# A first half of the next unit's hidden product, and an output tile, placed between two block products of a fused attention and two-MoE kernel

## The chip, the cores and the metric

One NeuronCore of a Trainium2 chip runs the whole program. The metric is the device time of one execution in microseconds (us); the median of three runs of the kernel before is 636.27 us.

## The reference, cut to what matters

The program is three layers in a row: banded attention (a plain and a dilated window), a mixture of four experts, and a layer with a rational activation. The change lies in the second layer:

```python
def _moe_ref(x, domain_probs, w1, w2):
    N, D = x.shape                       # 1152 tokens, 512
    E = w1.shape[0]                      # 4 experts, 1024 hidden each
    p = domain_probs / (domain_probs.sum(-1, keepdims=True) + 1e-09)
    out = np.zeros((N, D), dtype=np.float32)
    for e in range(E):
        h = np.maximum(x @ w1[e], 0.0)
        out += p[:, e:e + 1] * (h @ w2[e])
    return out
```

## The kernel before, in words

The 4096 hidden values of the four experts are cut into 16 **units** of 256; two units make a **group** (`g` from 0 to 7, units `u = 2g` and `u + 1`). The 1152 tokens are three **chunks** of 384 (c = 0, 1, 2), or nine output tiles of 128 (t = 0 to 8; chunk c holds tiles 3c to 3c + 2). Every float32 factor is split into a high and a low part, and a product is three products: high by high, high by low, low by high.

For each unit and chunk the kernel forms a hidden product (128 hidden values by 384 tokens per PSUM bank, two banks), takes ReLU, and splits it into `hh` (ScalarE, L485) and `hl` (VectorE, L489). For each group and output tile it then multiplies `hh` and `hl` with both units' `w2` (an output tile, twelve matmuls of L513) and adds the result to `acc`: in most groups ScalarE scales the tile into `part` (L543) and a DMA issued by GpSimd adds it (L544); in the last group VectorE does both (L546).

**Chunk 0** of a unit is computed plainly: `h_paced` (L898) issues two banks with `h_bank` (L461, twelve matmuls of L467 each), then the ReLU. **Chunks 1 and 2 together** are computed from groups 1 on by seven block products instead of eight (a scheme in the manner of Strassen), in class `Blocks` (L924). Each block product is six matmuls of L935 and accumulates into PSUM. A unit has two PSUM tiles of two banks: `yz` for chunk 1 and `vz` for chunk 2. The steps are:

- `first` into `yz` bank 1, copied to bank 0 by ScalarE (L974); `fifth` into a bank of its own, copied to `p5` (L981); `sixth` onto `yz` bank 1;
- `sum_up`, which asks VectorE for the sum of `yz` bank 1 and `p5` into `vz` bank 0 (the add of L961);
- `seventh` onto `yz` bank 1, after which a second add of L961 writes `vz` bank 1 from `yz` bank 1 and `p5`;
- `second` onto `yz` bank 0; `third` onto `vz` bank 0, then the ReLU of chunk 2; `fourth` onto `yz` bank 1, then the ReLU of chunk 1.

The loop of L1023 writes the order of a group out by hand. Of the group's first unit, `a`, the second add is followed by `second` of `a`, then by `first` of the other unit, `b`, and only then by `third` and `fourth` of `a`. Of the second unit, `b`, the order is `fifth`, `sixth`, `sum_up`, output tiles 0, 1, 2 of this group (0 and 1 in group 7), `seventh`, `second`, `third`, `fourth`, with nothing between. The next group begins with both banks of chunk 0 for its first unit and the output tiles 6, 7, 8 of the group before.

TensorE's order is the program's. The other engines' work is woven in by a planner (class `Pace`, L756 to L806): each TensorE step advances a model clock with `passed` (L787) by its cost in `COST`; work with a due time (`later`), such as the adds and the low halves of the ReLU, is issued once the clock has passed it, and the gaps are filled with preparation (`behind`: splitting weights, forming sums of weight blocks) and with the conversion of the third layer's weights from float64. `settle` issues what a step needs before it goes on. Hidden PSUM tiles come from a pool of two (`psh`) or, where `last` is True, from a third one; output tiles take turns in two banks (`pso`). In the add of a unit:

```python
            def add(self, n, wait=0.2):
                out, y, p5 = self.place(n), self.place(1), self.p5
                later(
                    wait, COST["add"], ("add", self.u),
                    lambda: nc.vector.tensor_tensor(out=out, in0=y, in1=p5, op=ALU.add),
                )
```

After group 7 a list written out by hand, `DENSE`, orders the third layer.

Of the kernel before, what the change touches and what calls it, by code (L numbers as in the profile page):

```python
# [95 lines left out]
COST = dict(h=2.09, p=1.045, o=2.74, osum=0.78, relu=1.0, add=0.59, split=0.68, sums=0.42, bits=0.41, both=1.15, token=1.0)  # L96
# [5 lines left out]
def body(ctx, tc, qkv, mask, dp, w1, w2, w1d, w2d, coef, out):  # L102
# [15 lines left out]
    def h_tile(last=None):  # L118

        count[0] += 1  # L120
        last = third and count[0] % 3 == 0 if last is None else last
        pool = third[0] if last else psh
        return pool.tile([128, 2, 512], F32, tag="h", name="ps_h")
# [67 lines left out]
    def weight(store, u, n):  # L191

        return (store[u][:, i].rearrange("p (k f) -> p k f", k=n) for i in range(2))
# [267 lines left out]
    def h_bank(u, c, i, ps, ks=range(4)):  # L461
        wh, wl = weight(w1s, u, 4)
        xh, xl = xt[c]
        for k in ks:
            f = slice(i * 128, (i + 1) * 128)
            for n, (a, b) in enumerate(((wh, xh), (wh, xl), (wl, xh))):
                nc.tensor.matmul(  # L467
                    ps[:, i, :TC], lhsT=a[:, k, f], rhs=b[:, k],
                    start=k + n == 0, stop=k + n == 5,
                )  # L470
# [46 lines left out]
    def o_bank():  # L517
        return pso.tile([128, 512], F32, tag="o", name="ps_o")
# [41 lines left out]
    class Rational:  # L560
# [53 lines left out]
        def high(self):  # L614
            self.hh, self.hl = new_h(self.u, self.c)
            nc.scalar.copy(self.hh, self.u1)  # L616
# [6 lines left out]
    with tc.manual_schedule():  # L623
# [73 lines left out]
        def fill(u, c, i):  # L697
            if i == 0:
                ps_h[u, c] = h_tile()
            h_bank(u, c, i, ps_h[u, c])  # L700
# [6 lines left out]
        def small_loads():  # L707
# [9 lines left out]
            g=small_loads,  # L717
# [44 lines left out]
        def run_due(n=0):  # L762
            ready, cost, _, f = Pace.due.pop(n)
            Pace.dv = max(Pace.dv, ready) + cost if cost else Pace.dv
            f()

        def run_prep():
            ready, cost, _, f = Pace.prep.pop(0)
            Pace.dv = max(Pace.dv, ready) + cost if cost else Pace.dv
            f()  # L770
# [16 lines left out]
        def passed(us):  # L787

            Pace.pe += us
            while Pace.due and min(Pace.due)[0] <= Pace.pe:  # L790
                n = Pace.due.index(min(Pace.due))
                fill(Pace.due[n][0])
                run_due(n)
            fill(Pace.pe)

        def later(wait, cost, key, f):
            Pace.due.append((Pace.pe + wait, cost, key, f))

        def settle(key):
            while any(d[2] == key for d in Pace.due):  # L800
                run_due(Pace.due.index(min(Pace.due)))
            while any(d[2] == key for d in Pace.prep):
                run_prep()

        def behind(cost, key, f, wait=0.0):
            Pace.prep.append((max(Pace.pe, Pace.dv) + wait, cost, key, f))  # L806

        def act_then(key, act, low, cost):

            def both():  # L810
                act()
                n, dv = 0, 0.0
                while not Pace.conv[0] and n < len(Pace.prep) and dv < 1.0 and Pace.prep[n][1]:
                    dv += Pace.prep[n][1]
                    n += 1
                Pace.prep.insert(n, (Pace.dv + 1.0, cost, key, low))
            return both
# [70 lines left out]
        def tokens_later(src, high, low, key="tokens", then=None):  # L888
# [6 lines left out]
                    then()  # L895
            behind(0.0, key, act_then(key, act, dve, COST["token"]))

        def h_paced(u, c, last=None):  # L898
            settle(("w1", u))
            ps = h_tile(last)  # L900
            for i in range(2):
                h_bank(u, c, i, ps)
                passed(COST["h"])
            high, low = relu_parts(u, c, ps)
            high()
            later(1.1, COST["relu"], ("h", u, c), low)

        def o_paced(g, t, wait=0.0):
            for v in range(2):
                settle(("h", 2 * g + v, t // 3))  # L910
                settle(("w2", 2 * g + v))
            ps = o_bank()
            for v in range(2):
                o_half(g, t, v, ps)
            passed(COST["o"])
            if by_dma(g, t):
                if wait:
                    later(wait, 0.0, ("o", g, t), lambda: o_sum(g, t, ps))
                else:
                    o_sum(g, t, ps)  # L920
            else:
                later(0.2, COST["osum"], ("o", g, t), lambda: o_sum(g, t, ps))
# [100 lines left out]
        for g in range(NG1):  # L1023
            u = 2 * g
            again = g + 1 in BLOCKED
            o = lambda *at: [(o_paced, *i) for i in at]
            if g == 0:
                later(0.0, COST["osum"], ("o", 0, 3), lambda: o_sum(0, 3, ps_2[3]))
                token_sums()
                tokens_later(temp[0], *(t[:, 0] for t in tt))  # L1030
                sums_later(2)
                sums_split_later(2, 1)
                o_paced(0, 4)
                o_paced(0, 5)
                for v in range(2):
                    h_paced(v, 2)
                tokens_later(temp[2], *(t[:, :2] for t in xt[2]), "first")
                sums_split_later(2, 0)
                tokens_later(temp[1], *(t[:, 1] for t in tt), "second")
                sums_later(3)  # L1040
                tokens_later(temp[3], *(t[:, 2] for t in tt), "third", begin_conversion)
                continue
            a, b = (Blocks(v) for v in (u, u + 1))
            w2_loads = (load_w2, u + 2), (load_w2, u + 3)
            free = [(load_w1, u + 3)] * (g > 1) + [w2_loads[0]] * (g == 1) + [w2_loads[1]]
            free = [(weights_free, *free)] if again else []
            run = lambda g, *ts: [o_paced(g, t, 1.5 * (n == 2)) for n, t in enumerate(ts)]

            def next_sums():
                if again:  # L1050
                    sums_later(u + 2)
                    sums_split_later(u + 2, 1)
                    split_later(w2s, "w2", u + 2)
                    split_later(w1s, "w1", u + 3)
                else:
                    loads((load_w1, u + 3))

            if g == 1:
                sums_split_later(u + 1, 1)
                split_later(w1s, "w1", u + 2)  # L1060
                a.first(False)
                o_paced(0, 6)
                a.sixth()
                a.fifth()
                a.sum_up(0.8, False)
                o_paced(0, 7)
                a.seventh()
                a.second()
                sums_split_later(u + 1, 0, free)
                o_paced(0, 8)  # L1070
            else:
                for v in (u, u + 1):
                    new_h(v, 0)
                h_paced(u, 0, False)
                sums_split_later(u + 1, 1)
                split_later(w2s, "w2", u + 1)
                if again:
                    split_later(w1s, "w1", u + 2)
                run(g - 1, 6, 7, 8)
                a.first(False)  # L1080
                h_paced(u + 1, 0, True)
                a.fifth()
                a.sixth()
                a.sum_up(0.2, False)
                run(g - 1, 3, 4)
                sums_split_later(u + 1, 0, free)
                o_paced(g - 1, 5, 1.5)
                a.seventh()
                a.second()
            b.first(True)  # L1090
            a.third()
            a.fourth()
            next_sums()
            b.fifth()
            b.sixth()
            b.sum_up(0.2, False)
            run(g, *range(3 if again else 2))
            b.seventh()
            b.second()
            b.third()  # L1100
            b.fourth()
            if g == 1:
                Window.spare[:] = [None, lone[:, 0], lone[:, 1]]
            if again:
                sums_split_later(u + 2, 0, [(loads, (load_w1, u + 4))])
                sums_later(u + 3)
            else:
                loads(*w2_loads, (load_w1, u + 4), (load_w1, u + 5))
# [144 lines left out]
        def of(name):  # L1253
# [3 lines left out]
            h=bank, o=second, O=lambda *a: second(*a, of="h"), z=sum_up, x=turn, X=x_high, Y=x_low, W=x_whole,  # L1257
# [5 lines left out]
            i=load_w1, j=load_w2, k=load_sums,  # L1263
# [112 lines left out]
```

## Time and profile before

| | |
|---|---|
| median of 3 runs | 636.27 us (635.47 to 637.51) |
| the profiled execution | 636.8 us |
| its span, first to last instruction | 635.0 us |
| mean granted TensorE clock | 0.999 of full speed |
| TensorE matmul busy | 622.0 us, 98% of the span |
| VectorE busy | 522.6 us, 82% |
| ScalarE busy | 371.5 us, 58% |
| GpSimd busy | 88.1 us, 14% |

Times in the rows are from the start of the span; the profiled execution is 1.8 us longer than its span. PE is TensorE's matmul, PEld its weight load, DVE VectorE, ACT ScalarE, POOL GpSimd, SP SyncE (SPq is its DMA queue). A line such as L961 is the line of the kernel that issued the instruction.

### The profile page before, as it was taken

What the parts mean: (1) busy time and instruction counts of PE and PEld (TensorE: products, weight loads), DVE (VectorE), ACT (ScalarE), POOL (GpSimd) and SP (SyncE); (2) the same over time, 40 slices, a digit from 0 to 9 for tenths busy, and PEclk for the clock granted to TensorE, in tenths of its full rate; (3) what the DMA queues carried; (4) which work ended last, traced back from release to release, by engine and by line L of the source; (5) the groups of instructions that cost most, each with busy time, mean ns of one, the idle gap of its engine ahead of it and who ended that gap; (6) DMA issues with size and microseconds to landing.
All of it is one profiled execution on the core that took longest, in us unless ns stands there. A gap on an engine that the chain in (4) does not pass through costs nothing.

```text
span 635.0 us, 9851 instructions
## 1 busy us (share of the span) xinstructions
PE 622.0 (98%) x3726; PEld 554.6 (87%) x3728; DVE 522.6 (82%) x788; ACT 371.5 (58%) x682; POOL 88.1 (14%) x103
## 2 busy tenths in 40 slices
PE   7999999999999999999999999999999999999997
PEld 4888898899899899899899889888998889899886
DVE  7687488789888888888898888438898899899894
ACT  6787625355554554464555555127688686877760
POOL 2223330011111112112112111000000002111110
PEclk9999999999999999999999999999999999999999
DMA  9965302259778869879868878950331563572333
GB/s 264 311 171 168 111 11 67 100 138 258 230 214 239 242 196 265 239 211 247 253 188 244 248 207 225 316 199 10 124 133 38 180 212 95 116 239 51 67 78 105
DMA packets 39535, 111.28 MB, mean 175 GB/s; under 512 B 4256, under 2 KB 5024, under 8 KB 37440
## 3 DMA queue, kind: packets, MB, share of 16 engines
q1 hardware_dynamic: 29104, 92.14, 43.9%
q0 software_dynamic: 9936, 18.09, 16.3%
q8 instruction: 29, 0.48, 0.3%
q10 hardware_dynamic: 448, 0.43, 0.3%
q14 instruction: 18, 0.15, 0.1%
HBM read 67.13 MB, written 25.43 MB: 146 GB/s over the span
## 4 chain that ended last, share of the span: by engine, by line
PE 97%; DVE 1%; DMA 1%; ACT 0%; issue 0%
PE ps_o L513 45%; PE ps_h L467 21%; PE ps_h L935 14%; PE ps_h L1232 7%; PE ps_o L935 2%; PE ps_v L431 2%; PE ps_s L417 1%; PE ps_h L513 1%; DMA qk<-in_qkv_dram 1%; PE ps_s L362 1%; PE ps_h L1166 1%; DVE ps_h L961 1%; PE ps_h L655 1%; PE ps L362 0%; DVE xl L893 0%
## 5 line engine op out<-in xcount | busy, mean ns | idle before, releaser
L513 PE MATMUL ps_o<-w,hh 128*128 128x512 f32 (+1 forms) x848 | 228.7, 391 | 0.3 <-DVE xl L455 0.3
L513 PEld LDWEIGHTS ps_o<-w,hh 128*128 128x128 f32 x848 | 157.0, 188 | 29.8 <-DVE xl L455 0.7
L513 PE MATMUL ps_o<-w,hl 128*128 128x512 f32 (+1 forms) x424 | 131.0, 390 | 0.1
L467 PE MATMUL ps_h<-xh,w 128*128 128x384 f32 x464 | 125.2, 338 | 0.0
L513 PEld LDWEIGHTS ps_o<-w,hl 128*128 128x128 f32 x424 | 79.4, 188 | 17.6 <-DVE hl L489 0.6
L467 PEld LDWEIGHTS ps_h<-xh,w 128*128 128x128 f32 x464 | 84.4, 188 | 1.0
L544 POOL DMA_DIRECT2D acc<-part x51 | 45.1, 884 | 264.0 <-ACT part L543 262.1
L467 PE MATMUL ps_h<-xl,w 128*128 128x384 f32 x232 | 77.7, 335 | 0.0
L543 ACT ACTIVATE part<-ps_o,p_sb 128x512 f32<-128x512 f32 x51 | 35.1, 688 | 54.8 <-PE ps_o L513 24.3
L485 ACT ACTIVATE hh<-ps_h 128x768 fp32r<-128x768 f32 x48 | 38.9, 812 | 41.0 <-PE ps_h L935 22.8
L489 DVE SCALAR_TENSOR_TENSOR hl<-ps_h,hh 128x768 fp32r<-128x768 f32 x48 | 45.4, 953 | 12.7 <-ACT hh L485 11.9
L467 PEld LDWEIGHTS ps_h<-xl,w 128*128 128x128 f32 x232 | 43.6, 188 | 0.4
L1151 POOL DMA_DIRECT2D acc<-part x18 | 15.6, 867 | 200.3 <-ACT part L1150 199.7
L271 ACT ACTIVATE x<-x 128x512 f32<-128x512 f32 x32 | 21.8, 681 | 21.4 <-DVE t L268 21.4
L935 PE MATMUL ps_h<-t,sw 128*128 128x384 f32 x168 | 34.0, 337 | 0.0
L833 DVE TENSOR_TENSOR w<-raw,w 128x512 fp32r<-128x512 f32 x48 | 32.8, 683 | 0.9 <-ACT w L829 0.9
L396 ACT ACTIVATE pr<-pr,mx 128x80 f32<-128x80 f32 (+1 forms) x84 | 29.8, 358 | 5.9 <-DVE mx L390 4.6
L935 PEld LDWEIGHTS ps_h<-t,sw 128*128 128x128 f32 x168 | 29.9, 188 | 1.2
L580 DVE SCALAR_TENSOR_TENSOR sq<-sq,absb,ab 128x768 f32<-128x768 f32 x24 | 24.2, 1013 | 7.9 <-ACT sq L569 6.7
L935 PE MATMUL ps_h<-xh,w 128*128 128x384 f32 x104 | 29.8, 336 | 0.0
L829 ACT CAST w<-raw 128x512 fp32r<-128x512 f32 x48 | 28.6, 614 | 0.0
L616 ACT CAST hh<-u 128x768 fp32r<-128x768 f32 x24 | 19.9, 838 | 13.4 <-DVE u L610 13.2
(158 smaller groups left out, 1132.2 us busy)
## 6 DMA issues: line engine op xcount, KB each, us to landing
acc<-part POOLq DMA_DIRECT2D x69, 256.0 KB, 5.5
raw<-in_w_dram SPq DMA_DIRECT2D x32, 512.0 KB, 6.3
w<-w SPq DMA_DIRECT2D x14, 1024.0 KB, 6.1
w<-lone SPq DMA_DIRECT2D x18, 512.0 KB, 4.9
x<-in_w1d_dram SPq DMA_DIRECT2D x16, 512.0 KB, 5.1
x<-in_w2d_dram SPq DMA_DIRECT2D x16, 512.0 KB, 5.2
w<-w SPq DMA_DIRECT2D x14, 512.0 KB, 4.5
sw<-sw SPq DMA_DIRECT2D x12, 512.0 KB, 7.5
```

The costliest lines, as they stand in the source:

```text
L396: nc.scalar.activation(pr[:, j, i], pr[:, j, i], AF.Exp, scale=-1.0, bias=self.mx[:, j, i:i + 1], accum_out=self.total[:, j, i:i + 1],)
L467: nc.tensor.matmul(ps[:, i, :TC], lhsT=a[:, k, f], rhs=b[:, k], start=k + n == 0, stop=k + n == 5,)
L485: nc.scalar.activation(hh, ps[:, :, :TC], AF.Relu)
L489: nc.vector.scalar_tensor_tensor(out=hl, in0=ps[:, :, :TC], scalar=0.0, in1=hh.bitcast(F32), op0=ALU.max, op1=ALU.subtract,)
L513: nc.tensor.matmul(ps, lhsT=a[:, i, tk], rhs=b[:, i, cols], start=v + n == 0, stop=v + n == 6)
L543: nc.scalar.activation(part, ps, AF.Copy, scale=pe)
L544: nc.gpsimd.dma_start(acc[t], part, accum_op=ALU.add)
L580: nc.vector.scalar_tensor_tensor(out=self.sq, in0=self.sq, scalar=absb[:, 1:2], in1=self.ab, op0=ALU.mult, op1=ALU.add,)
L829: nc.scalar.copy(store[u][:, 0, s_], raws[nm, u][:, s_])
L833: nc.vector.tensor_tensor(out=w[:, 1, s_], in0=raws[nm, u][:, s_], in1=w[:, 0, s_].bitcast(F32), op=ALU.subtract)
L935: nc.tensor.matmul(out, lhsT=a[i][:, k], rhs=b[j][:, k], start=first and k + n == 0, stop=k + n == 3, skip_group_check=not first,)
L1232: nc.tensor.matmul(out, lhsT=a[i][:, k], rhs=b[j][:, k], start=first and k + m == 0, stop=k + m == 3, skip_group_check=not first,)
```

## The change

The two banks of `h_paced` can now be issued apart: a new `h_begin` issues bank 0, and `h_paced` issues only bank 1 where bank 0 was begun before. In groups 1 to 6 bank 0 of chunk 0 of the next group's first unit (twelve matmuls) is issued between `second` and `third` of unit `b`; the next group's `h_paced` then issues bank 1, the ReLU as before. In group 7, which has no next group, output tile 1 stands between `second` and `third` of `b`, instead of ahead of `seventh`.

```diff
+        begun = {}
+
+        def h_begin(u, c, last=None):
+            settle(("w1", u))
+            begun[u, c] = h_tile(last)
+            h_bank(u, c, 0, begun[u, c])
+            passed(COST["h"])
+
         def h_paced(u, c, last=None):
-            settle(("w1", u))
-            ps = h_tile(last)
-            for i in range(2):
-                h_bank(u, c, i, ps)
-                passed(COST["h"])
+            if (u, c) not in begun:
+                h_begin(u, c, last)
+            ps = begun[u, c]
+            h_bank(u, c, 1, ps)
+            passed(COST["h"])
             high, low = relu_parts(u, c, ps)
@@
             b.sum_up(0.2, False)
-            run(g, *range(3 if again else 2))
+            run(g, *range(3 if again else 1))
             b.seventh()
             b.second()
+            if again:
+                h_begin(u + 2, 0, False)
+            else:
+                o_paced(g, 1)
             b.third()
             b.fourth()
```

`again` is true in groups 1 to 6.

## Rows read from the trace of the kernel before

**Rows 1.** The page: busy time of the engines, and the granted clock over the span.
```profile
PE 622.0 (98%) x3726; PEld 554.6 (87%) x3728; DVE 522.6 (82%) x788; ACT 371.5 (58%) x682; POOL 88.1 (14%) x103
...
PEclk9999999999999999999999999999999999999999
```

**Rows 2.** What PE waited for: us in total, times, longest us.
```profile
PE ps_h L935 <- DVE ps_h L961: 4.6, 7, 0.7
PE ps_s L362 <- DMA qk<-in_qkv_dram: 1.4, 1, 1.4
```

**Rows 3.** The chain that ended last, groups 3 and 7: start, us, what.
```profile
168.62 2.12 PE ps_h L935 x12
171.38 2.38 PE ps_h L935 x12
173.76 4.16 PE ps_h L467 x24
177.92 8.20 PE ps_o L513 x36
...
408.65 2.12 PE ps_h L935 x12
411.42 2.38 PE ps_h L935 x12
413.79 4.13 PE ps_o L513 x18
```

**Rows 4.** Busy time of each engine in one group's period, stage windows.
```profile
171.38:219.90 48.52, 47.86 (x240) 43.21 (x241) 42.32 (x74) 25.52 (x42) 8.13 (x10) 1.00 0.84 238
```

**Rows 5.** Timeline of group 3 around third of unit b: start, us, what.
```profile
170.39 0.34 PE L935 MATMUL ps_h<-xh,w 128*128 128x384 f32 x1
...
170.76 0.57 DVE L961 TENSOR_TENSOR ps_h<-ps_h,p 128x384 f32<-128x384 f32 x1 [1.84 <-PE ps_h L935]
...
171.38 0.45 PE L935 MATMUL ps_h<-xh,sw 128*128 128x384 f32 x1 [0.66 <-DVE ps_h L961]
...
172.76 0.82 ACT L485 ACTIVATE hh<-ps_h 128x768 fp32r<-128x768 f32 x1 [2.04 <-PE ps_h L935]
...
173.60 2.00 DVE L489 SCALAR_TENSOR_TENSOR hl<-ps_h,hh 128x768 fp32r<-128x768 f32 x2 [0.63 <-ACT hh L485]
...
179.15 1.08 PE L513 MATMUL ps_o<-w,hh 128*128 128x512 f32 x4
```

**Rows 6.** Timeline, second add of unit a in groups 2 to 7, two following thirds.
```profile
155.25 0.57 DVE L961 TENSOR_TENSOR ps_h<-ps_h,p 128x384 f32<-128x384 f32 x1 [0.65 <-PE ps_h L935]
...
203.77 0.57 DVE L961 TENSOR_TENSOR ps_h<-ps_h,p 128x384 f32<-128x384 f32 x1 [0.38 <-PE ps_h L935]
...
252.26 0.57 DVE L961 TENSOR_TENSOR ps_h<-ps_h,p 128x384 f32<-128x384 f32 x1 [0.33 <-PE ps_h L935]
...
253.11 0.33 PE L935 MATMUL ps_h<-xh,sw 128*128 128x384 f32 x1
...
300.78 0.57 DVE L961 TENSOR_TENSOR ps_h<-ps_h,p 128x384 f32<-128x384 f32 x1 [1.59 <-PE ps_h L935]
...
349.30 0.57 DVE L961 TENSOR_TENSOR ps_h<-ps_h,p 128x384 f32<-128x384 f32 x1 [0.48 <-PE ps_h L935]
...
398.10 0.56 DVE L961 TENSOR_TENSOR ps_h<-ps_h,p 128x384 f32<-128x384 f32 x1
...
398.71 0.45 PE L935 MATMUL ps_h<-xh,sw 128*128 128x384 f32 x1
```

**Rows 7.** What DVE and ACT waited for between 90 and 425 us.
```profile
DVE hl L489 <- ACT hh L485: 10.8, 15, 2.3
...
DVE w L245 <- ACT w L241: 6.0, 6, 2.2
DVE lone L245 <- ACT lone L241: 4.9, 5, 1.5
...
ACT part L543 <- DMA acc<-part: 14.5, 5, 5.3
```

**Rows 8.** Timeline of group 7: its output sums on DVE, the SP loads behind fourth.
```profile
408.69 0.75 DVE L546 SCALAR_TENSOR_TENSOR acc<-ps_o,p_sb,acc 128x512 f32<-128x512 f32 x1 [1.97 <-PE ps_o L513]
...
413.82 0.32 SPq L152 DMA_DIRECT2D w<-w  x1
```

## The prediction

> **What bounds the kernel now.** I read the page's busy times first: TensorE is busy for 98% of the span, the next engine, VectorE, for 82%, and the clock is at its upper level (2.4 GHz) in every slice [rows 1]. So the time is TensorE's work plus what TensorE waits for. The list of its waits has only one entry that is not in the attention stage: block products wait for the add of L961 seven times, 4.6 us in all [rows 2]. To see which product, I took the chain of waits: in group 3 a run of two block products is followed by a gap and two more, and then by chunk 0 of the next unit [rows 3]. The timeline names them: `second` of unit b issues its last matmul at 170.39; the add starts at 170.76, just after that matmul's end; `third` starts at 171.38 [rows 5]. Seven waits, one in each of groups 1 to 7, always `third` of b. Unit a has the same steps but `first` of b stands in between as cover, and there the add is hidden [rows 6].
>
> **What one wait costs.** The list shows 0.66 us of idleness, but the pipeline also has to run empty and fill again, so I price it by the chain. From the start of the chain's pair `seventh`, `second` to the end of `fourth` are 24 matmuls: 173.76 - 168.62 = 5.14 us, and in group 7 413.79 - 408.65 = 5.14 us too. The next 24 matmuls of the same shape, with no wait among them, take 4.16 us [rows 3]. One wait costs 5.14 - 4.16 = 0.98 us. A check from the other side: one period from `third` to the next `third` is 48.52 us for 240 matmuls [rows 4]. Nine output tiles are 108 of them, at 8.20/36 us; 132 are left at 4.16/24 us [rows 3]: 24.60 + 22.88 = 47.48 us. That leaves 1.04 us of loss, 0.98 of it at this place, and 0.06 us for all other changes of bank and operand in a group.
>
> The Trainium skill, on its page "TensorE: Matmul & The Clock Gate", section "Single matmul latency", gives an isolated warm matmul as (398 + N)/2.4 ns and a matmul in a row as N/2.4 + 2.5 ns: about 0.16 us for a restart. An estimate by it is 7 x (0.66 + 0.16) = 5.7 us to win. The chain's 0.98 us is 0.32 us above the idleness, twice that; I go by the chain.
>
> **The change, part by part.**
>
> *Groups 1 to 6.* The twelve matmuls of bank 0 are moved, not added: 12 x 4.16/24 = 2.08 us of work in front of `third`. The add keeps its place in the program: it falls due 0.2 us after `seventh`, and the clock has passed that once `second` is counted, so it is issued before the new bank. It then ends and frees `third` about 0.62 us after its start (171.38 - 170.76), and 2.08 us cover that with 1.4 us to spare. Gain: 6 x 0.98 = 5.88 us. More accumulators in turn on TensorE: between nothing and the 0.06 us per group above; I take nothing.
>
> *Group 7.* Output tile 1, 8.20/3 = 2.73 us, covers the same add: another 0.98 us. In its old place only tile 0 is left between `sixth` and `seventh`, which hides the first add; that add needs the same 0.62 us against 2.73, so nothing is lost. Tile 1's own sum, 0.75 us on VectorE [rows 8], moves behind the second add. The weight loads on SP stay behind `fourth` [rows 8], with the same TensorE work ahead. The sum of both parts: 7 x 0.98 = 6.86 us at most.
>
> *What the moved step passes.* It issues no DMA. SP's and POOL's queues hold the same transfers in the same order among those the change writes out; POOL is busy for 8.13 us of 48.52 and ACT for 25.52 [rows 4]. The weights of the new bank were split at the beginning of the group, and its PSUM tile is that of unit a's chunk 2, whose ReLU lies four block products or more and three output tiles back. So the early bank waits for nothing. The DMA engines' share of 0.84 [rows 4] rises with a period of 47.54 us to 0.86.
>
> *The ReLU of b's chunk 2.* It is issued after `third` as before, but only one bank, not two, now stands between `fourth` and output tile 6, which reads it in its second half. In group 3 that half begins at 179.15; `hh` is done at 173.58 and the first `hl` near 174.6 (half of 2.00 us) [rows 5]: 4.5 us of margin, 2.08 less after the change, 2.5 us left. Cost: nothing, with ACT and VectorE as the cover.
>
> *What is late next.* VectorE has to do the same work in a period 0.98 us shorter. It meets TensorE at the second add of unit a. There it waits 0.65, 0.38, 0.33, 1.59 and 0.48 us in groups 2 to 6; in group 7 it comes late already [rows 6]. `third` of a gives it a little more: an add starting at 252.26 would allow 252.88, and `third` starts at 253.11, so 0.23 us. If VectorE never caught up, the new stalls would be 0.98 less the wait less 0.23: 0.10, 0.37, 0.42, 0 and 0.27 us, and the whole 0.98 in group 7: 2.14 us. Four of them would be new and pay a restart, 0.98 - 0.66 = 0.32 us each: 1.28 us. Together 3.42 us. The other end is no loss: VectorE waits for ACT 10.8 + 6.0 + 4.9 us in these groups [rows 7], about 3 us in each, and much of that follows TensorE (ACT's ReLU and the casts behind it) and comes earlier when TensorE does. I take 0.8 us: half of group 7's 0.98, which has no wait to give, and 0.3 us for the others.
>
> **Sum.** 6.86 - 0.8 = 6.06 us. The profiled execution took 636.8 us, so 630.7 us in its terms; the median of the runs shown is 0.5 us lower, 636.27, and gives **630.2 us**, 0.95% less. About 0.3% (1.9 us) is what a measurement here can tell from no change.
>
> **The rivals.**
>
> *VectorE carries the lateness over.* The stall of b is gone, but unit a's `third` stalls instead, by up to 3.42 us in all. For it: the thin 0.23 us and the late add of group 7 [rows 6]. Against it: VectorE's waits for ACT. Time: 636.27 - 6.86 + 3.42 = 632.8 us.
>
> *The wait moves along with the cover.* The add of L961 did not start when `seventh` was done, though it reads only what `seventh` wrote; it started when `second` was done [rows 5]. Should it be released by whatever matmul stands last before `third`, it would wait for the new bank too, `third` would wait as before, and the time stays at 636.3 us. Against it: in unit a `first` of b stands last before `third`, and the add at 252.26 is through while `third` follows at 253.11 without a gap of that size [rows 6]. This is also the case in which the change doesn't do what it says.
>
> *Slower: ACT is late with `hh`.* Place: output tile 6 of the next group, with its margin down from 4.5 to 2.5 us. ACT waits five times, up to 5.3 us, until a DMA has read the tile `part` [rows 7]; one such wait ahead of the ReLU makes `hh` late. Price: the excess over 2.5 us, 2.8 us for the longest. The change is lost only if ACT is 2.5 + 6.86/6 = 3.6 us late in each of six groups. With the longest wait in all six it is 636.27 - 6.86 + 16.8 = 646.2 us. Against it: the five average 2.9 us, and TensorE waited for none of them.
>
> **How the numbers follow.** Forecast 0.70; VectorE's carry-over in full 0.16; the wait that moves along 0.08; the slower case 0.06. The first two are faster by over 0.3%: 0.86; the third is within it: 0.08; the last is slower: 0.06. The range begins where all 6.86 us arrive, 629.4 us, less 0.6 us for the spread of runs, and ends at the carry-over's 632.8 us plus 0.8 us for it: 628.8 to 633.6 us.
>
> **What would show it.** Right: no `third` of b among TensorE's waits; the seven pieces of four block products lose their gap; the add of b still starts right after `second`, beside the new bank; the period from one `third` of b to the next is 47.5 to 47.7 us; small waits for L961 only at `third` of a, in group 7 first. Wrong: the add of b starting after the new bank's twelve matmuls; waits for L961 of 0.3 us or more in most groups' unit a; or output tiles waiting for `hh` or `hl`.

## The result, and the profile after

The changed kernel takes 629.19 us (median of 4 runs, 628.63 to 629.52) against 636.41 us before: a ratio of 0.9885, 95% interval 0.9867 to 0.9903. Forecast was 630.2 us in a range of 628.8 to 633.6. Line numbers behind the edit move by 8 or 12: the block products' L935 is now L943, the adds' L961 is L969 (a little further in some of the experiments).

The rows of the kernel before that are headed or called group 3 between 168 and 180 us [rows 3, 5] are those of group 2, and the period that starts at 171.38 us [rows 4] runs from `third` of b in group 2 to that in group 3: unit a's second add of group 2 starts at 155.25 us, that of group 3 at 203.77 us [rows 6]. The numbers are not touched by this. Below, each group has its own number.

The page, the longest entries of the list of what TensorE waited for, and one period from `third` to `third` of unit b (stage windows; the columns of [rows 4]):

```profile
PE 620.5 (99%) x3728; PEld 555.2 (88%) x3728; DVE 522.5 (83%) x788; ACT 372.3 (59%) x682; POOL 88.1 (14%) x103
...
PEclk9999999999999999999999999999999999999999
```
```profile
PE ps_h L655 <- DVE warm L645: 1.2, 1, 1.2
PE ps_s L362 <- DMA qk<-in_qkv_dram: 0.6, 1, 0.6
PE ps_o L513 <- DVE xl L455: 0.3, 1, 0.3
```
```profile
171.10:218.66 47.56, 47.56 (x242) 43.22 (x241) 40.46 (x71) 25.56 (x42) 8.04 (x9) 1.00 0.82 226
```

TensorE's seven waits for the add [rows 2] are gone, and all that is left lies in the first 78 us, ahead of groups 1 to 7. The period fell from 48.52 [rows 4] to 47.56 us, and TensorE is busy through all of it; the clock is unchanged. The chain of group 2 and of group 7 (start, us, what) has no gap left:

```profile
166.92 2.10 PE ps_h L943 x12
169.02 2.08 PE ps_h L467 x12
171.10 2.08 PE ps_h L943 x12
173.18 2.08 PE ps_h L467 x12
175.26 8.20 PE ps_o L513 x36
...
399.28 2.10 PE ps_h L943 x12
401.38 2.76 PE ps_o L513 x12
404.14 2.10 PE ps_h L943 x12
```

Each piece starts where the one before it ends; in the chain that is the end of the last matmul of the piece before. In [rows 3] the second piece of block products started 0.64 us after the end of the first. The timeline of group 2, to be held against [rows 5]:

```profile
168.69 0.33 PE L943 MATMUL ps_h<-xh,w 128*128 128x384 f32 x1
...
169.06 0.57 DVE L969 TENSOR_TENSOR ps_h<-ps_h,p 128x384 f32<-128x384 f32 x1 [1.87 <-PE ps_h L943]
...
170.94 0.33 PE L943 MATMUL ps_h<-xh,sw 128*128 128x384 f32 x1
...
172.18 0.82 ACT L485 ACTIVATE hh<-ps_h 128x768 fp32r<-128x768 f32 x1 [3.19 <-PE ps_h L943]
...
173.12 1.90 DVE L489 SCALAR_TENSOR_TENSOR hl<-ps_h,hh 128x768 fp32r<-128x768 f32 x2
...
176.49 1.08 PE L513 MATMUL ps_o<-w,hh 128*128 128x512 f32 x4
```

The add starts 0.37 us after the start of `second`'s last matmul, as before, and runs beside the new bank; `third` starts at 170.94, 1.3 us after the add's end. `hh` of chunk 2 is done at 173.00 and the first `hl` near 174.1; output tile 6 reads them from 176.49 on.

**Where the time went.** The part ahead of group 1's output tiles took between 110.2 and 112.1 us in the profiled executions of kernels whose program is the same up to there, and would blur a comparison of spans. So all kernels are compared over a stretch of the chain of their one profiled execution: from the first output tile of group 1 to the first transposes of the third layer. Before, and after:

```profile
111.89 8.20 PE ps_o L513 x36
...
395.68 5.40 PE ps_h L935 x30
...
417.92 1.31 PE ps_h L1166 x12
```
```profile
111.16 8.20 PE ps_o L513 x36
...
389.21 5.22 PE ps_h L943 x30
...
410.38 1.31 PE ps_h L1178 x12
```

417.92 - 111.89 = 306.03 us before, 410.38 - 111.16 = 299.22 us after: 6.81 us won in the stretch. The spans differ by 7.5 us (635.0 and 627.5); of the rest, 0.73 us lie ahead of the stretch, in code that is the same, and the part behind it is equal, 213.0 us to the end of the last matmul.

The middle rows show unit a's `third` in group 7: its late add [rows 6] cost 0.18 us before (5.40 against 5.22 us). That is not the change's gain. In e2 below the program is the one of the kernel before up to this point, and there the piece takes 5.22 us as well. The two executions differ in a wait of VectorE for a load from HBM a little earlier; before, and in e2:

```profile
385.80 0.43 DVE L258 TENSOR_SCALAR t<-x 128x512 uint32<-128x512 uint32 x1 [1.35 <-DMA x<-in_w1d_dram]
```
```profile
384.35 0.43 DVE L258 TENSOR_SCALAR t<-x 128x512 uint32<-128x512 uint32 x1 [0.20 <-DMA x<-in_w1d_dram]
...
396.94 0.57 DVE L969 TENSOR_TENSOR ps_h<-ps_h,p 128x384 f32<-128x384 f32 x1 [0.20 <-PE ps_h L943]
```

So 0.18 us of the stretch before belong to that one execution. The seven stalls of b account for 6.81 - 0.18 = 6.63 us, 0.95 us each; one period against the other gives the same price, 48.52 - 47.56 = 0.96 us.

### The profile page after: what moved, and what is told of

Read it like the earlier page. It is cut to its first block, busy times and chain, and to the rows that moved or that the text cites. A ratio compares the mean times of both kernels' runs of the same rounds, so it can differ in the third digit from the quotient of the medians.

```text
span 627.5 us, 9852 instructions
## 1 busy us (share of the span) xinstructions
PE 620.5 (99%) x3728; PEld 555.2 (88%) x3728; DVE 522.5 (83%) x788; ACT 372.3 (59%) x682; POOL 88.1 (14%) x103
## 4 chain that ended last, share of the span: by engine, by line
PE 97%; DMA 1%; DVE 1%; ACT 0%; issue 0%
PE ps_o L513 46%; PE ps_h L467 22%; PE ps_h L943 14%; PE ps_h L1244 7%; PE ps_o L943 2%; PE ps_v L431 2%; PE ps_s L417 1%; PE ps_h L513 1%; DMA qk<-in_qkv_dram 1%; PE ps_s L362 1%; PE ps_h L1178 1%; PE ps_h L655 1%; PE ps L362 0%; DVE xl L893 0%; PE ps_h L362 0%; DVE hl L489 0%
## 5 line engine op out<-in xcount | busy, mean ns | idle before, releaser
L969 DVE TENSOR_TENSOR ps_h<-ps_h,p 128x384 f32<-128x384 f32 x28 | 15.9, 566 | 23.2 <-PE ps_h L943 23.2
L943 PE MATMUL ps_h<-t,sw 128*128 128x384 f32 x168 | 34.0, 337 | 0.0
L943 PEld LDWEIGHTS ps_h<-t,sw 128*128 128x128 f32 x168 | 29.9, 188 | 1.2
L943 PE MATMUL ps_h<-xh,w 128*128 128x384 f32 x104 | 29.7, 335 | 0.0
```

The lines of the kernel that those rows point to most:

```text
L943: nc.tensor.matmul(out, lhsT=a[i][:, k], rhs=b[j][:, k], start=first and k + n == 0, stop=k + n == 3, skip_group_check=not first,)
```

## The experiments

The first eight are the kernel before with a part or a variant of the change; group 7 is as before unless it is said. e9 is the kernel after with one edit, e10 the kernel before with one. "Stretch" is the one defined above; 0.18 us of every difference to the kernel before is that kernel's own late add in group 7. The ratios are medians of all runs against the kernel before on the same chip.

| kernel | stretch, us | against before | ratio of runs, 95% interval |
|---|---|---|---|
| before | 306.03 | | |
| after | 299.22 | -6.81 | 0.9885 [0.9867, 0.9903] |
| e1_groups | 300.11 | -5.92 | 0.9897 [0.9878, 0.9916] |
| e2_last | 304.94 | -1.09 | 0.9987 [0.9975, 0.9999] |
| e3_tensor_only | 300.11 | -5.92 | 0.9915 [0.9897, 0.9933] |
| e4_planner_only | 305.84 | -0.19 | 0.9996 [0.9986, 1.0006] |
| e5_three | 302.55 | -3.48 | 0.9939 [0.9924, 0.9953] |
| e6_six | 300.11 | -5.92 | 0.9911 [0.9897, 0.9926] |
| e7_after_third | 305.85 | -0.18 | 0.9997 [0.9987, 1.0006] |
| e8_before_second | 300.12 | -5.91 | 0.9900 [0.9886, 0.9915] |
| e9_bare_a | 304.98 | -1.05 (+5.76 to after) | 0.9986 [0.9976, 0.9995] |
| e10_add_at_once | 313.90 | +7.87 | 1.0137 [1.0114, 1.0160] |

Four kernels with the same stretch to 0.01 us (e1, e3, e6, e8) have medians from 629.56 to 630.97 us; that difference lies outside the stretch, and no run shows where in the runs that were not profiled.

**The two halves.** e1 keeps the diff's `h_begin` and drops group 7; e2 does the opposite:

```diff
-            run(g, *range(3 if again else 1))
+            run(g, *range(3 if again else 2))     # e1
             b.seventh()
             b.second()
             if again:                             # e2: if not again:
-                h_begin(u + 2, 0, False)          # e2
-            else:                                 # e1
-                o_paced(g, 1)                     # e1
```

> The early bank in groups 1 to 6 alone, group 7 as before. Theory (the bank covers the add, 0.98 us at each of six places): 636.4 - 5.9 = 630.5 us, one wait of TensorE for the add left, in group 7, of 0.66 us. Rival (the early bank wins less and the gain of the whole is from group 7): 633 us or more, with more than one such wait.

> Output tile 1 between second and third in group 7 alone, groups 1 to 6 as before. Theory: one place, 0.98 us, 635.4 us, six waits for the add left, 4.0 us in the list. Rival (the sums of the output tiles or the third layer's start come late): 636.4 us or more although the wait of group 7 is gone.

e1 took 629.56 us with one wait of 0.7 us left, e2 635.13 us with six of 4.0 us in all. Both agree with the theory, and the halves add up: without the 0.18 us, e1 won 5.74 us, 0.96 us at each of six places, and e2 0.91 us at one, together 6.65 against 6.63 us. e2's interval ends at 0.9999, so by its runs alone it would hardly be told from no change; the stretch and the missing wait show it.

**Order on TensorE or order on VectorE?** The early bank also advances the planner's clock, and so VectorE, ScalarE and SyncE get their work in another order. e3 moves the bank and leaves the clock; e4 moves the clock and leaves the bank (both shown against the changed kernel's `h_begin`).

```diff
         def h_begin(u, c, last=None):       # e3
             settle(("w1", u))
             begun[u, c] = h_tile(last)
             h_bank(u, c, 0, begun[u, c])
-            passed(COST["h"])               # now in h_paced, ahead of bank 1
         def h_begin(u, c, last=None):       # e4
             settle(("w1", u))
-            begun[u, c] = h_tile(last)
-            h_bank(u, c, 0, begun[u, c])    # now in h_paced, ahead of bank 1
+            begun[u, c] = last
             passed(COST["h"])
```

> TensorE's order of e1_groups with the queues of VectorE, ScalarE, SyncE and GpSimd in exactly the order of the kernel before: the planner's clock is advanced only where it was before. Theory (the cover alone makes the gain, and VectorE's waits for ScalarE give way): 630.5 us as in e1_groups, no third of unit a waiting for more than 0.3 us. Rival (VectorE's order was needed too: the low halves of the ReLU now stand in its queue 2.08 us before their input, and the lateness reaches the second add of unit a): 633 us or more, waits for the add at third of unit a in most groups.

> The other half: TensorE's order of the kernel before with the queues of the other four engines in the order of e1_groups. Theory: third of b still has no cover, 0.98 us at each of seven places stay, 636.4 us. Rival (the new order of VectorE brought part of the gain): below 634 us with fewer than seven waits.

e3 took 630.97 us and e4 636.01 us. The stretch of e3 is that of e1 to the hundredth, and e4's is the one of the kernel before without its 0.18 us, with all seven waits: the whole gain comes from TensorE's order, and VectorE's new order alone brings nothing. (By the medians e3 is 1.4 us slower than e1; the stretch does not have that difference.) What VectorE waited for in e3 between 90 and 418 us (us in total, times, longest) and its second add of unit a in group 3:

```profile
DVE ps_h L969 <- PE ps_h L943: 13.4, 15, 1.8
DVE hl L489 <- ACT hh L485: 12.4, 12, 2.3
...
DVE w L245 <- ACT w L241: 4.6, 4, 2.7
...
DVE lone L245 <- ACT lone L241: 2.2, 3, 0.9
```
```profile
200.73 0.57 DVE L969 TENSOR_TENSOR ps_h<-ps_h,p 128x384 f32<-128x384 f32 x1 [0.39 <-PE ps_h L943]
```

That add waited 0.38 us before [rows 6] and 0.39 us now, in a period 0.96 us shorter: there VectorE is not later. Over this part of the kernel it waits as long for the adds as before (13.4 us against 13.6), a little longer for `hh` (12.4 against 10.8), and 4.1 us less for the casts of L241 (6.8 against 10.9 [rows 7]).

**How much cover is needed.** e5 and e6 issue only 3 or 6 of the twelve matmuls early (the planner's clock gets the same shares of the cost, not shown):

```diff
         def h_begin(u, c, last=None):
-            h_bank(u, c, 0, begun[u, c])
+            h_bank(u, c, 0, begun[u, c], range(1))     # e6: range(2)
         def h_paced(u, c, last=None):
+            h_bank(u, c, 0, ps, range(1, 4))           # e6: range(2, 4)
             h_bank(u, c, 1, ps)
```

> As e1_groups, but only three of the twelve matmuls (0.52 us) stand between second and third in groups 1 to 6; the other nine follow fourth. Theory (the cover works by its length: third is free 0.82 us after its place in an unbroken row, and a stall costs 0.16 us more for the restart): 0.30 + 0.16 = 0.46 us of each 0.98 stay, 6 x 0.52 = 3.1 us won, 633.2 us, with waits for the add of about 0.14 us at six places and 0.66 in group 7. Rival (any work of TensorE there frees third): 630.4 us. Rival (the gain goes with the share of the bank): 634.8 us.

> As e1_groups, but six of the twelve matmuls (1.04 us) between second and third. Theory: 1.04 us is more than 0.82, so the whole 5.9 us is won as with twelve, 630.4 us, one wait left, in group 7. Rival (the gain goes with the share of the bank): 633.4 us. Rival (six are too thin, since VectorE comes late to the add in some groups): between the two, with waits for the add in those groups.

e6 took 630.5 us, the whole gain with half the cover. e5 took 632.21 us: 3.48 us less the 0.18 of group 7 is 0.55 us at each of six places, against 0.52 expected. Its period, and its timeline in group 2:

```profile
169.70:217.66 47.96, 47.83 (x240) 43.18 (x240) 40.83 (x71) 25.85 (x42) 8.08 (x10) 1.00 0.79 226
```
```profile
169.08 0.57 DVE L971 TENSOR_TENSOR ps_h<-ps_h,p 128x384 f32<-128x384 f32 x1 [1.83 <-PE ps_h L945]
...
169.22 0.34 PE L467 MATMUL ps_h<-xh,w 128*128 128x384 f32 x1
...
169.69 0.19 PEld L945 LDWEIGHTS ps_h<-xh,sw 128*128 128x128 f32 x1 [0.45 <-DVE ps_h L971]
169.70 0.44 PE L945 MATMUL ps_h<-xh,sw 128*128 128x384 f32 x1
```

Of each stall 47.96 - 47.56 = 0.40 us stays, but TensorE counts as idle for only 47.96 - 47.83 = 0.13 us of the period, near the 0.14 expected. The list of waits has no entry that short and shows only the wait of group 7; the weight load's row and the period show the stall.

**The place.** e7 puts the bank between `third` and `fourth`, e8 between `seventh` and `second`:

```diff
             b.seventh()
+            if again: h_begin(u + 2, 0, False)     # e8
             b.second()
             b.third()
+            if again: h_begin(u + 2, 0, False)     # e7
             b.fourth()
```

> As e1_groups, but the early bank stands one block product later, between third and fourth. Theory (only what stands ahead of third covers the add): nothing won, 636.3 us, seven waits of 0.66 us. Rival (the split of chunk 0's product, or the later ReLU, helps by itself): below 634 us.

> As e1_groups, but the early bank stands one block product earlier, between seventh and second, so that the add is issued ahead of second. Theory (the add waits for the last matmul on its tile issued before it): the add starts right behind seventh, beside the bank, third is free, the whole 5.9 us is won, 630.4 us. Rival (it is released by the matmul that stands last ahead of third): the add starts behind second, third waits 0.66 us as before in all seven groups, 636.3 us.

e7 took 635.79 us with seven waits, 4.6 us in all: the same work one product later wins nothing. e8 took 629.9 us, and its timeline in group 2 settles what releases the add:

```profile
166.85 0.33 PE L467 MATMUL ps_h<-xh,w 128*128 128x384 f32 x1
...
167.05 0.57 DVE L969 TENSOR_TENSOR ps_h<-ps_h,p 128x384 f32<-128x384 f32 x1 [0.82 <-PE ps_h L943]
```

The bank follows `seventh` from 166.85, and the add starts 0.20 us later, with `second` still 2 us away. In the kernel before it waited for `second` because `second` had been issued ahead of it, onto the tile that the add reads. Here the bank has been issued ahead of it too (the planner asks for the add only after the bank), but into another tile, and the add does not wait for it.

**The same stall elsewhere.** e9 is the changed kernel with unit a's cover taken away:

```diff
-            b.first(True)
             a.third()
+            b.first(True)
             a.fourth()
```

> The changed kernel with unit a's cover taken away: third of a ahead of first of b, fourth behind it, in groups 1 to 7. Theory (the same add without cover costs the same at any place): seven new stalls of 0.98 us, 629.3 + 6.9 = 636.2 us, seven waits of 0.66 us at third of a. Rival (unit a's stall is smaller, as VectorE is ahead there, or larger, as it is late): 633 or less, 638 or more.

e9 took 634.89 us, with six waits, not seven. The seven was a miscount: in group 1 output tile 8 stands between `second` and `third` of a already and covers the add. Six stalls cost 5.76/6 = 0.96 us each by the stretch, the price of b's.

**By tile or by bank?** `third` has no datum in common with the second add: it writes bank 0 of `vz`, the add bank 1. e10 issues the add at once behind `seventh` in the kernel before, and moves nothing on TensorE:

```diff
                 self.product(self.place(1), self.summed(0, 0), self.t(1))
                 self.add(3)
+                settle(("add", self.u))
```

> The kernel before with one thing changed: the second add is issued directly after seventh in both units, ahead of second; no bank and no output tile is moved. It reads bank 1 of yz and writes bank 1 of vz; second writes bank 0 of yz, third bank 0 of vz, so no data is shared with either. Theory (matmuls and the add wait for each other by tile, not by bank): second now waits for the add, in unit a too where it was covered, 14 stalls of 0.98 us, 7 more than before: 636.0 + 6.9 = 642.9 us. Rival (the waits go by bank, and only the order of issue tied the add to second): second runs beside the add, its 1.04 us cover the 0.82, and the whole gain comes without moving a bank: 629.2 us, no wait for the add.

e10 took 645.08 us, 9.5 us more than the kernel before (635.61 us on its chip). TensorE's wait in its list, and the timeline of unit b in group 2 and unit a in group 3:

```profile
PE ps_h L935 <- DVE ps_h L961: 11.8, 14, 1.3
```
```profile
171.07 0.57 DVE L961 TENSOR_TENSOR ps_h<-ps_h,p 128x384 f32<-128x384 f32 x1 [0.79 <-PE ps_h L935]
...
171.69 0.19 PEld L935 LDWEIGHTS ps_h<-xh,w 128*128 128x128 f32 x1 [0.98 <-DVE ps_h L961]
171.69 0.44 PE L935 MATMUL ps_h<-xh,w 128*128 128x384 f32 x1 [0.66 <-DVE ps_h L961]
...
204.62 0.56 DVE L961 TENSOR_TENSOR ps_h<-ps_h,p 128x384 f32<-128x384 f32 x1
...
205.24 0.44 PE L935 MATMUL ps_h<-xh,w 128*128 128x384 f32 x1 [1.22 <-DVE ps_h L961]
```

Fourteen waits, now at `second`, which writes bank 0 of `yz` while the add reads bank 1. With the bank of another tile that ran beside the add in e8 and after the change, this shows that the program's waits go by tile. The excess over the expected 6.9 us is VectorE's lateness: the add at 204.62 did not wait for TensorE but for VectorE's own queue, and the idleness behind it is 1.22 us, not 0.66. Over all fourteen the idleness is 11.8 us against 14 x 0.66 = 9.2 us, 2.6 us more, which is the excess. The stretch shows less (+7.87 us), as one of the seven new stalls, unit a's in group 1, lies ahead of it. Two tiles of one bank each, in place of one of two, might free `third` without any move; that was not run.

## Why the prediction was right, point by point

*The bound and the price.* Right. TensorE's own work and seven waits for the add of L961 set the time of these groups. The price from the chain, 0.98 us, measured 0.95 to 0.96 us (stretch, period, e9). The idleness of the list, 0.66 us, would have given 4.6 us for seven; 6.63 us were won.

The rows of [rows 5], with the matmul that follows, and those after the change take the price apart:

```profile
171.38 0.19 PEld L935 LDWEIGHTS ps_h<-xh,sw 128*128 128x128 f32 x1 [0.98 <-DVE ps_h L961]
...
171.67 0.34 PE L935 MATMUL ps_h<-xl,sw 128*128 128x384 f32 x1
```
```profile
170.77 0.33 PE L467 MATMUL ps_h<-xh,w 128*128 128x384 f32 x1
170.77 0.19 PEld L943 LDWEIGHTS ps_h<-xh,sw 128*128 128x128 f32 x1
...
170.94 0.33 PE L943 MATMUL ps_h<-xh,sw 128*128 128x384 f32 x1
...
171.12 0.33 PE L943 MATMUL ps_h<-xl,sw 128*128 128x384 f32 x1
```

In an unbroken row the next matmul starts 0.17 us after the one ahead (170.77, 170.94), although each is shown for 0.33 us. Before, `third` started 171.38 - 170.39 = 0.99 us after the last matmul of `second`: 0.82 us late. Its second matmul then came 0.29 us after the first instead of 0.18: 0.11 us more. Together that is 0.93 of the 0.96 us. The list gives 0.66 us since it counts from the end of the matmul ahead, 0.16 us behind the place where the next could have started.

The Trainium skill's estimate of 5.7 us lies below the 6.63 us too. Its page "TensorE: Matmul & The Clock Gate" has the formula for one warm matmul in section "Single matmul latency" and the one for matmuls in a row in "Back-to-back issue gap"; their difference, the estimated 0.16 us for a restart, is worked out for bf16 matmuls and agrees with the 0.16 us between end and place here (the profile models where a matmul ends, so this is no second measurement of it). The 0.11 us of the first matmul behind the wait are not in it.

*What the moved step passes.* Right. The early bank waits for nothing and the add keeps its place; e7 and e8 show that the cover has to stand ahead of `third` and that its place on the near side of `second` does not matter. Group 7's two moves cost next to nothing: e2 won 0.91 of its 0.98 us. The DMA engines' share in the period did not rise to 0.86 but was 0.82; in these groups TensorE waited for no DMA.

*The ReLU's margin.* Right: the first `hl` is ready 2.4 us ahead of tile 6's second half, against 2.5 forecast, and TensorE waits for none. ACT's waits for the DMA that reads `part` fell from 14.5 us [rows 7] to 2.4 us, so the slower rival never came near; in e3 they were 13.8 us, and TensorE did not wait for `hh` there either.

*What is late next.* This is the term that was mis-sized: 0.8 us was taken for VectorE's lateness at unit a's second add, and it was zero. The forecast won 6.06 us and the medians differ by 7.22 us. Of the 1.16 us between them this term gave 0.8; the seven stalls, at 6.63 in place of 6.86 us, took back 0.2; the other 0.6 us lie outside the stalls, and no term of the forecast accounts for them. 629.19 us lies near the fast end of the range, which had been set for a charge of nothing.

Half of it, 0.5 us, was taken for group 7, where the add "comes late already". That lateness was no property of the kernel but of the one execution that was profiled, with its wait of 1.35 us for a load (shown with the result). In e2, with the same program up to there, the add waits for TensorE for 0.20 us.

The other 0.3 us, for the groups before, were not needed either. e3 is the test, with the bank moved and VectorE's order as before: the same add waits for 0.32 us or more in groups 2 to 6 and for 0.30 us in group 7, so VectorE keeps up with the shorter period; its waits for the casts give way (6.8 against 10.9 us). In the full change VectorE even waits longer at those adds than before, and so comes earlier (adds of groups 2, 3 and 7; then what VectorE waited for between 90 and 418 us):

```profile
153.55 0.57 DVE L969 TENSOR_TENSOR ps_h<-ps_h,p 128x384 f32<-128x384 f32 x1 [1.25 <-PE ps_h L943]
...
201.11 0.57 DVE L969 TENSOR_TENSOR ps_h<-ps_h,p 128x384 f32<-128x384 f32 x1 [1.45 <-PE ps_h L943]
...
391.35 0.57 DVE L969 TENSOR_TENSOR ps_h<-ps_h,p 128x384 f32<-128x384 f32 x1 [0.51 <-PE ps_h L943]
```
```profile
DVE ps_h L969 <- PE ps_h L943: 23.2, 21, 1.9
...
DVE hl L489 <- ACT hh L485: 2.6, 6, 0.5
```

These answer to [rows 6, 7]. This part is the planner's doing and not the cover's: e4, which has only the planner's new order, shows nearly the same waits (1.25, 1.45 and 0.52 us in groups 2, 3 and 7). The new order puts fillers ahead of the ReLU's low half, so the waits for `hh` fell from 10.8 to 2.6 us, and it leaves less of the conversion to these groups. From `third` of b in group 1 to that in group 6 VectorE ran 365 operations (210.5 us) before and 353 (203.7 us) after, with the rest mostly in group 7 and behind. The forecast took its work in a period as fixed.

The bound of 3.42 us, for a VectorE that never catches up, was not reached in any group. That its lateness does cost TensorE where the add has no cover is shown by e10 alone.

*The rivals.* The wait that moves along with the cover is refuted by e8: the add is tied to what was issued ahead of it, not to what stands last before `third`. But its premise was sound: the add did wait for `second` without needing its data, and e10 shows the same tie in the other direction. VectorE's carry-over did not occur: no `third` of unit a is among TensorE's waits after the change.

## What to carry to other kernels

Price a stall from the period or the chain, against the same instructions in an unbroken row, and not from the idleness that a list of waits gives: here 0.96 us against 0.66, and stalls of 0.40 us did not appear in TensorE's list at all. Before a wait in one profiled execution is taken for a property of the kernel, look for it in a second one: the late add of group 7 was in one only. Cover for a short dependent operation has to be as long as the operation's way there and back (here `third` came 0.82 us late; 1.04 us of matmuls won everything, 0.52 us a little over half) and has to stand ahead of the instruction that waits, from work that shares no tile with it. Where two banks of one tile are used independently, look at the order of issue: a wait may be there for the tile's sake, with no datum behind it.

## What the runs showed of the hardware that was not expected

The first matmul behind a wait took 0.44 to 0.45 us, its neighbours 0.33 to 0.34, and its weight load started with it (171.38 for both in [rows 5] and the row above, 171.69 for both in e10) instead of ahead of it, where in an unbroken row the load starts 0.17 us earlier (170.77 and 170.94 us after the change). The matmul behind it followed after 0.29 us (0.27 in e5) instead of 0.17 to 0.18. These 0.10 to 0.11 us and the 0.16 us by which the list's idleness starts too late make up most of the 0.3 us that a stall costs beyond that idleness; in e5, 0.13 us of idleness stood for a stall of 0.40 us in the same way. That the late weight load is the reason for the slower first matmul is likely but not shown.
